# A causal attention and two feed-forward layers on one core: a reordered opening with its softmax sums on TensorE

## The chip, the cores and the metric

The program runs on one NeuronCore of a Trainium2 chip. The metric is the device time of one execution in microseconds (us). The engines are named as in the profile: PE is TensorE (matmuls; PEld its weight loads), DVE is VectorE, ACT is ScalarE, POOL is GpSimd, SP is SyncE, which issues the DMAs.

## What is computed

Two sequences (B = 2) of 576 tokens with 8 heads of 64 columns go through attention with a memory, then through two feed-forward layers. Cut to what matters here:

```python
scores = where(causal, -1e9, q @ k.T / 8)
a = exp(scores - scores.max(-1))
local = (a / (a.sum(-1) + 1e-9)) @ v
phi = lambda x: where(x > 0, x, exp(x) - 1) + 1
mem_out = (phi(q) @ M_prev) / (phi(q) @ z_prev + 1e-6)
g = 1 / (1 + exp(-beta))
x = g * mem_out + (1 - g) * local
x = relu(x @ w_in)**2 @ w_out
out = sum over e of p[:, e] * (relu(x @ w1[e]) @ w2[e])
```

## The kernel before

The 1152 tokens lie in nine tiles of 128. They go through the attention in three chunks: chunk 0 holds the first 128 tokens of both sequences (tiles 7 and 8), chunk 1 four tiles, chunk 2 three. The work is staged. The **opening** (function `opening`, called once) computes the attention of chunk 0 whole. Then the first feed-forward layer of chunk 0 (`ffn1(0, ...)`) runs on TensorE with the attention of chunk 1 mixed in between its products (`rest`), then that layer for chunk 1 with the attention of chunk 2, then for chunk 2, and last the four experts.

In the opening and in the stage behind it every engine takes its instructions in the order in which the code issues them. In the opening that order is one string of step names, which `opening` walks through: `c` is a step of the weight conversion, `s0`/`s1` steps of the scores of heads 0 to 3 and 4 to 7, `p0`/`p1` of the feature map phi, `g` of the gates, `m` the products with the memory, `t` the transposition of a block of Exps with its copy out of PSUM, `v` the product with the values, `n`, `k`, `q`, `x`, `o` the normalisation, weighing, addition and transposition into the layer's input, `S` the first scores of chunk 1, `w` the first step of the layer. A block (unit) is one sequence and four heads, 128 queries by 128 keys per head, so there are four blocks.

A head's scores come from PSUM with the mask added and the row maximum taken by VectorE (`top`, L189); ScalarE then takes the Exp of 128 columns at a time (L324) and writes the row sum beside it with `accum_out`, which is an instruction of its own in the trace (ACTIVATION_READ_ACCUMULATOR). VectorE copies three of the four transposed blocks out of PSUM (L339), ScalarE the fourth (L341). phi is one Exp on ScalarE and two operations on VectorE (L181, L183, L184). The weights are the reciprocal of the sums times one minus the gate (L424 to L426), for all heads at once; the weighing (L432) and the addition of the memory's part (L433) go by sequence.

The opening shares ScalarE, VectorE and SyncE with the weight conversion (`convert`): the first layer's weights arrive as 64-bit words, 512 KB per block (`fetch`, L722), ScalarE makes two halves of the number (L734, L737), VectorE joins them (L740, L745), and the result `bits` goes both to TensorE and to a buffer in DRAM (L748). SyncE takes its issues in order, so the load of a later block stands behind the write of an earlier one:

```python
def fetch(i):
    words[i] = wp.tile([P, DM, 2], I32, tag=f"w{i % 2}", name="w64")
    nc.sync.dma_start(out=words[i]..., in_=w1[f, half]...)
...
    nc.sync.dma_start(out=w1s[f, half], in_=bits.bitcast(F32))
```

The first product of the layer (L101, `hpa<-y,bits`) needs both sequences' outputs of the opening (`y`, copied by L438) and the first converted block.

Of the kernel before, what the change touches and what calls it, by code (L numbers as in the profile page):

```python
# [10 lines left out]
F32 = mybir.dt.float32  # L11
# [5 lines left out]
AF = mybir.ActivationFunctionType  # L17
# [4 lines left out]
P = 128  # L22
B, H, S, D = 2, 8, 576, 64
# [14 lines left out]
CHUNKS = [(7, 9), (0, 4), (4, 7)]  # L38
# [14 lines left out]
def attention_then_experts(ctx, tc, qa, ka, va, qc, kc, vc, mz, beta, w1, probs, w2, out):  # L53
# [11 lines left out]
    nc = tc.nc  # L65
# [104 lines left out]
    def gates():  # L170
# [59 lines left out]
    def opening(c0, c1, first_layer):  # L230

        sc = [c0.scores(p, spot) for p, spot in zip(c0.pairs, (("s", 3), ("pv", 2)))]
        ph, gt, later = c0.phis(0), gates(), c1.scores(c1.pairs[0])
        units = [u for p in c0.pairs for u in p]
        steps = dict(
            g=lambda: next(gt), c=lambda: next(cv), w=lambda: next(first_layer), l=lambda: [c1.load(1, n) for n in range(2)], L=lambda: c1.load(1, 2), S=lambda: next(later, None),
            n=c0.norms, k=c0.recall, q=c0.weights,
        )
        for i in range(2):
            steps[f"s{i}"] = lambda i=i: next(sc[i], None)  # L240
            steps[f"p{i}"] = lambda i=i: next(ph[i])
            steps[f"x{i}"] = lambda i=i: c0.local(i)
            steps[f"o{i}"] = lambda i=i: c0.out(i)
        for i, u in enumerate(units):
            steps[f"t{i}"] = lambda u=u, e=nc.vector if i < 3 else None: c0.turn(u, e)
            steps[f"v{i}"] = lambda u=u: c0.values(u)
        for i in range(3):
            steps[f"m{i}"] = lambda i=i: c0.states(i)


        order = (
            "c l c L s0 p0 p0 g g p1 s1 s0 s0 s0 s1 s1 p1 m0 t0 s1 t2 s0 s1 m1 m2 n t1 v0 v2 k q x0 "
            "t3 c v1 v3 S o0 x1 o1 c S S c w S S S"
        )
        for k in order.split():
            steps[k]()

    def attention_a(c, pool, eng, banks):


        pairs = []
# [22 lines left out]

        def phis(r):
            e = q[r][1] = pool.tile([P, H, P], F32, tag="phia", name="phia", bufs=2)
            return [phi(e[:, hs], e[:, hs], q[r][0][:, hs]) for hs in (slice(0, 4), slice(4, 8))]

        def s_(pair, spot=None):
            scs = {}  # L290
            tag, bufs = spot or ("s", banks[1])
            for u in pair:
                t, kn, h0, nh = u
                b = TILES[t][0][0]
                if h0 + b == 0:
# [48 lines left out]
        def v_(u):  # L344
            t, kn, h0, nh = u
            b = TILES[t][0][0]
            at = at_.pop(u)
# [47 lines left out]
            b = TILES[t][0][0]  # L395
            finish(t, xls[t - b][:, b], banks[0], banks[2])()

        pms, fs = [], [pool.tile([P, B, H], F32, name=f"f{i}", bufs=1) for i in range(2 * (c == 0))]
        third = (slice(0, 3), slice(3, 6), slice(6, 8))

        def states(i):
            ps, tag, bufs = (banks[0], "m", banks[2]) if i < 2 else (ps_h, "h", 1)
            pms.append(ps.tile([P, 3, B, D + 1], F32, tag=tag, name="pm", bufs=bufs))
            for k, h in enumerate(range(third[i].start, third[i].stop)):
                nc.tensor.matmul(pms[i][:, k], lhsT=q[0][1][:, h, :], rhs=mzd[:, h], start=True, stop=True)

        def norms():
            for pm, hs in zip(pms, third):
                n = hs.stop - hs.start
                nc.vector.tensor_scalar_add(fs[1][:, :, hs], pm[:, 0:n, :, D].rearrange("p h b -> p b h"), 1e-6)  # L410
            nc.vector.reciprocal(out=fs[1], in_=fs[1])
            nc.vector.tensor_mul(fs[1], fs[1], gate[:, None, :].to_broadcast([P, B, H]))

        def recall():
            for pm, hs in zip(pms, third):
                n = hs.stop - hs.start
                nc.vector.tensor_mul(
                    q[0][2][:, :, hs, 0:D].rearrange("p b h d -> p h b d"), pm[:, 0:n, :, 0:D],
                    fs[1][:, :, hs].rearrange("p b h -> p h b")[:, :, :, None].to_broadcast([P, n, B, D]),
                )  # L420

        def weights():
            for b in range(B):
                nc.vector.tensor_scalar_add(fs[0][:, b], st[CHUNKS[0][0] + b][2], 1e-9)  # L424
            nc.vector.reciprocal(out=fs[0], in_=fs[0])
            nc.vector.tensor_mul(fs[0], fs[0], gate1[:, None, :].to_broadcast([P, B, H]))  # L426

        def local(b):
            xl = xls[b] = pool.tile([P, H, D], F32, tag="xl0", name="xl0", bufs=2)
            for i in range(2):  # L430
                hs = slice(4 * i, 4 * i + 4)
                nc.vector.tensor_mul(xl[:, hs], pvs[CHUNKS[0][0], i][:, b], fs[0][:, b, hs, None].to_broadcast([P, 4, D]))  # L432
            nc.vector.tensor_add(xl, xl, q[0][2][:, b, :, 0:D])  # L433
# [809 lines left out]
```

## Time and profile before

| | |
|---|---|
| time, median of 3 runs | 689.8 us (689.16 to 690.34) |
| the profiled execution's own time | 696.75 us |
| its span | 694.6 us |
| busy share of the span | PE 96%, PEld 70%, DVE 74%, ACT 64%, POOL 20% |
| first product of the layer (end of the opening) | 21.72 us |

The span runs from the first to the last instruction of one profiled execution. A timeline row gives the start, the duration, the engine, the line of the program, the operation and what it writes and reads; in brackets stands how long the engine stood idle before it, and what ended that. TensorE's records are passes: an fp32 matmul shows as two, a transposition as one.

### The profile page before, as it was taken

The page shows a single profiled execution, that of the slowest core. Times are in us where ns is not written, and L with a number is a line of the kernel's source. Part 1 is how long each engine was busy: PE and PEld are TensorE (multiplying, and loading weights), DVE is VectorE, ACT ScalarE, POOL GpSimd, SP SyncE. Part 2 cuts the span into 40 slices and gives each one's busy share as a digit, 9 for nine tenths or more (in the row PEclk, how much of TensorE's full clock was granted, in tenths as well). Part 3 has the DMA queues.
Part 4 walks back from the last instruction along what each step waited for, and adds up shares of the span by engine and source line. Part 5 has one row for each costly group of instructions (what it writes and reads, how often), then busy time and mean ns, then how long its engine had stood idle before and what let it go on. Part 6 is the DMA issues. An engine that isn't in the chain of part 4 may idle for free. (4 is left out here: it accounts for less than half of the span.)

```text
span 694.6 us, 12446 instructions
## 1 busy us (share of the span) xinstructions
PE 669.6 (96%) x4604; PEld 483.6 (70%) x4604; DVE 513.4 (74%) x1011; ACT 442.6 (64%) x830; POOL 141.6 (20%) x197
## 2 busy tenths in 40 slices
PE   7799999899999999999999999999999999999997
PEld 4588878677877879999766666656655555555553
DVE  7879787599996586779689679787765856665743
ACT  5689976798686448966888677545534435353430
POOL 1010010000000022004335443433332242423200
PEclk9999999999999999999999999999999999999999
DMA  8798875679955636965122332333341323000002
GB/s 292 259 345 299 283 264 171 210 210 254 259 130 129 120 86 215 328 213 156 62 91 92 122 122 69 127 110 122 107 136 62 103 81 96 25 1 1 1 1 76
DMA packets 65565, 101.24 MB, mean 146 GB/s; under 512 B 32673, under 2 KB 34977, under 8 KB 65505
## 3 DMA queue, kind: packets, MB, share of 16 engines
q1 hardware_dynamic: 65216, 100.32, 47.2%
q8 instruction: 36, 0.59, 0.3%
q14 instruction: 25, 0.20, 0.1%
q10 hardware_dynamic: 288, 0.14, 0.1%
HBM read 82.87 MB, written 10.75 MB: 135 GB/s over the span
## 5 line engine op out<-in xcount | busy, mean ns | idle before, releaser
L1115 PE MATMUL o<-w,g 128*128 128x512 f16 x864 | 216.9, 379 | 0.0
L1017 PE MATMUL pe<-xs,wu 128*128 128x256 f16 (+1 forms) x1344 | 196.2, 286 | 3.1 <-DVE u L1039 2.3
L1017 PEld LDWEIGHTS <-wu 128*128 128x128 f16 x1344 | 130.8, 98 | 72.1 <-issue 6.2
L1115 PEld LDWEIGHTS <-g 128*128 128x128 f16 x864 | 84.5, 98 | 67.7 <-issue 0.2
L1033 ACT ACTIVATE g<-h 128x512 f16<-128x512 f32 (+1 forms) x64 | 43.4, 678 | 106.8 <-DVE h L1039 100.6
L804 PE MATMUL y<-g,w 128*128 128x512 f32 (+1 forms) x384 | 88.9, 369 | 0.7 <-DVE w L84 0.7
L983 POOL TENSOR_TENSOR ws<-raw 128x256 f32<-128x256 f32 x32 | 24.6, 769 | 259.1 <-DVE wu L980 132.9
L804 PEld LDWEIGHTS y<-g,w 128*128 128x128 f32 x384 | 68.2, 188 | 8.0 <-DVE w L84 1.0
L1034 DVE SCALAR_TENSOR_TENSOR g<-h,g 128x512 f16<-128x512 f32 (+1 forms) x64 | 51.6, 806 | 23.3 <-ACT g L1033 23.0
L1039 DVE SCALAR_TENSOR_TENSOR u<-pe,p 128x256 f32<-128x256 f32 (+1 forms) x64 | 28.8, 451 | 37.4 <-PE pe L1017 35.9
L106 PE MATMUL hpb<-x,w 128*128 128x512 f32 x192 | 53.0, 411 | 1.2 <-DVE r L788 1.2
L84 DVE TENSOR_TENSOR w<-wraw,w 128x512 fp32r<-128x512 f32 x64 | 45.3, 715 | 10.5 <-ACT w L83 10.4
L1039 DVE SCALAR_TENSOR_TENSOR h<-pe,u 128x256 f32<-128x256 f32 (+1 forms) x64 | 29.0, 453 | 29.9 <-PE pe L1017 29.6
L83 ACT ACTIVATE w<-wraw 128x512 fp32r<-128x512 f32 x64 | 39.6, 625 | 17.7 <-PE y L804 10.5
L980 DVE SCALAR_TENSOR_TENSOR wu<-ws,wpow,wu 128x512 f16<-128x512 f32 x64 | 45.6, 750 | 1.9 <-ACT wu L991 1.9
L189 DVE CUSTOM_DVE_ANT_0 a<-sc,mask 128x384 f32<-128x384 f32 (+4 forms) x80 | 36.5, 479 | 14.1 <-PE sc L589 9.9
L925 DVE SCALAR_TENSOR_TENSOR w<-raw,wpow,w 128x1024 f16<-128x1024 f32 x32 | 41.4, 1294 | 1.8 <-ACT w L924 1.3
L106 PEld LDWEIGHTS hpb<-x,w 128*128 128x128 f32 x192 | 35.5, 193 | 9.8 <-DVE r L788 2.4
L991 ACT ACTIVATE wu<-ws,wpow 128x1024 f16<-128x1024 f32 x32 | 36.4, 1137 | 6.4 <-POOL ws L988 6.4
L985 ACT ACTIVATE wu<-raw,wpow 128x768 f16<-128x768 f32 x32 | 29.8, 932 | 13.4 <-PE pe L1017 11.5
L980 DVE SCALAR_TENSOR_TENSOR wu<-raw,wpow,wu 128x768 f16<-128x768 f32 x32 | 33.2, 1039 | 6.1 <-ACT wu L985 5.7
L924 ACT ACTIVATE w<-raw,wpow 128x1024 f16<-128x1024 f32 x32 | 36.3, 1134 | 0.0
(172 smaller groups left out, 1101.9 us busy)
## 6 DMA issues: line engine op xcount, KB each, us to landing
raw<-in_w SPq DMA_DIRECT2D x64, 512.0 KB, 3.7
w<-in_w SPq DMA_DIRECT2D x32, 512.0 KB, 5.4
wraw<-w1s SPq DMA_DIRECT2D x64, 256.0 KB, 3.2
w1s<-bits SPq DMA_DIRECT2D x32, 256.0 KB, 3.7
kraw<-in_kc SPq DMA_DIRECT2D x8, 576.0 KB, 4.8
vraw<-in_vc SPq DMA_DIRECT2D x8, 320.0 KB, 3.7
qraw<-in_qc SPq DMA_DIRECT2D x4, 512.0 KB, 4.6
out<-acc SPq DMA_DIRECT2D x7, 256.0 KB, 2.0
```

The costliest lines, as they stand in the source:

```text
L83: nc.scalar.activation(out=w[:, 0], in_=raw, func=AF.Copy)
L84: eng.tensor_sub(w[:, 1], raw, w[:, 0].bitcast(F32))
L106: nc.tensor.matmul(acc, lhsT=w[:, a, kk * P:(kk + 1) * P], rhs=xs_r[c][:, b, kk, :], start=(i == 0), stop=(i == 3 * NK - 1),)
L189: nc.vector.tensor_tensor_reduce(out=dst, in0=sc, in1=msk, op0=ALU.add, op1=ALU.max, scale=1.0, scalar=-3.0e38, accum_out=m)
L804: nc.tensor.matmul(yacc[d], lhsT=w[:, a, d * P:(d + 1) * P], rhs=g[:, b], start=(first and i == 0), stop=(last and i == 2),)
L925: nc.vector.scalar_tensor_tensor(out=w1, in0=x, scalar=s, in1=w0, op0=ALU.mult, op1=ALU.subtract)
L980: nc.vector.scalar_tensor_tensor(out=w[:, 1, ks], in0=x, scalar=s1, in1=w[:, 0, ks], op0=ALU.mult, op1=ALU.subtract)
L1017: nc.tensor.matmul(acc, lhsT=w[:, wa, k, kk * P:kk * P + P], rhs=x[:, xb, kk], start=(m == 0 and not onto), stop=(m == 5), skip_group_chec ...
L1033: nc.scalar.activation(out=g[:, 0], in_=hm, func=AF.Relu)
L1034: nc.vector.scalar_tensor_tensor(out=g[:, 1], in0=hm, scalar=0.0, in1=g[:, 0], op0=ALU.max, op1=ALU.subtract)
L1039: nc.vector.scalar_tensor_tensor(out=out, in0=acc, scalar=HID, in1=x, op0=ALU.mult, op1=ALU.add)
L1115: nc.tensor.matmul(outs[t], lhsT=gs[i, m][:, gb, r:r + P], rhs=wds[i, m][:, wa], start=(p == 0 and m == 0 and wa == gb), stop=(p == 3 and ...
```

## The change

Six things change, all in the opening.

1. **Sums.** The Exps of chunk 0 no longer write their row sums. The sums come from TensorE: for each head the transposed block of Exps is loaded as weights and multiplied with one column of ones (`sums`, steps `z0` and `z1`), 8 products per step. The 16 result columns lie at the end of the PSUM bank of the first memory product.
2. **phi.** `phi_first` computes phi(q) of chunk 0 as exp(-relu(-q)) + relu(q): three activations on ScalarE and one addition, which goes to GpSimd for both halves.
3. **Copies.** All four transposed blocks are copied out by ScalarE.
4. **Weights per half.** The weights and the weighing go by four heads and both sequences (`weights(i)`, `local(i)`), so the first half can be weighed before the second is summed.
5. **Additions.** The memory's part is added by sequence in a step of its own (`join`): sequence 0 on VectorE, sequence 1 on GpSimd.
6. **Order.** The string of steps is new: the gates stand first, both phi steps ahead of the Exps, and one more conversion ahead of the layer's input.

```diff
+    def phi_first(out, r, q, eng):
+        nc.scalar.activation(out=out, in_=q, func=AF.Relu, scale=-1.0)
+        nc.scalar.activation(out=out, in_=out, func=AF.Exp, scale=-1.0)
+        nc.scalar.activation(out=r, in_=q, func=AF.Relu)
+        yield
+        eng.tensor_add(out, out, r)
+        yield
...
-            steps[f"t{i}"] = lambda u=u, e=nc.vector if i < 3 else None: c0.turn(u, e)
+            steps[f"t{i}"] = lambda u=u: c0.turn(u)
...
-            "c l c L s0 p0 p0 g g p1 s1 s0 s0 s0 s1 s1 p1 m0 t0 s1 t2 s0 s1 m1 m2 n t1 v0 v2 k q x0 "
-            "t3 c v1 v3 S o0 x1 o1 c S S c w S S S"
+            "g g c s0 l c L p0 p1 p0 s1 s0 s0 s0 s1 s0 s1 m0 t0 p1 s1 m1 m2 n t1 s1 "
+            "v0 t2 v1 z0 q0 k x0 t3 c v2 v3 z1 q1 x1 y1 S y0 S c w o0 o1 S S c S S"
...
+                return [phi_first(e[:, hs], p[:, hs], q[r][0][:, hs], eng) for hs, eng in zip(halves, (nc.gpsimd, nc.gpsimd))]
...
-                        accum_out=sm[:, h0 + i:h0 + i + 1],
+                        accum_out=sm[:, h0 + i:h0 + i + 1] if c else None,
...
+        def sums(i):
+            for u in pairs[i]:
+                at, b = at_.pop(u), TILES[u[0]][0][0]
+                for h in range(4):
+                    nc.tensor.matmul(
+                        sms[CHUNKS[0][0]][:, b, 4 * i + h:4 * i + h + 1], lhsT=at[:, h * P:h * P + P], rhs=ones[:, 0:1],
+                        start=True, stop=True,
+                    )
...
+        def weights(i):
+            hs = slice(4 * i, 4 * i + 4)
+            cf = cfs[i] = pool.tile([P, B, 4], F32, tag="cg", name="cg", bufs=2)
+            nc.vector.tensor_scalar_add(cf, sms[CHUNKS[0][0]][:, :, hs], 1e-9)
+            nc.vector.reciprocal(out=cf, in_=cf)
+            nc.vector.tensor_mul(cf, cf, gate1[:, None, hs].to_broadcast([P, B, 4]))
+
+        def local(i):
...
+            nc.vector.tensor_mul(
+                xls[0][:, :, 4 * i:4 * i + 4], pvs[CHUNKS[0][0], i], cfs[i][:, :, :, None].to_broadcast([P, B, 4, D])
+            )
+
+        def join(b):
+            (nc.gpsimd if b else nc.vector).tensor_add(xls[0][:, b], xls[0][:, b], q[0][2][:, b, :, 0:D])
```

How the instructions stand is shown at three places. `x8` behind a row means eight such instructions in a row; what an instruction waits for stands in brackets.

TensorE, before, from the third block's transposition on (`atp` is a transposed block of Exps, `pv` the product with the values):

```order
L336 MATMUL atp<-ident,a 128x128 [waits Activation_49] x4
L356 MATMUL pv<-va_0_162,at 64x64 [waits DMAHW7_49,DVE_49]
L356 MATMUL pv<-va_0_162,at 64x64 x7
L356 MATMUL pv<-va_0_162,at 64x64 [waits DVE_49]
L356 MATMUL pv<-va_0_162,at 64x64 x7
L336 MATMUL atp<-ident,a 128x128 [waits PE_49,Activation_49]
L336 MATMUL atp<-ident,a 128x128 [waits Activation_49] x3
L356 MATMUL pv<-va_0_164,at 64x64 [waits DMAHW0_49,DVE_49]
L356 MATMUL pv<-va_0_164,at 64x64 x7
L356 MATMUL pv<-va_0_164,at 64x64 [waits DVE_49,Activation_49]
L356 MATMUL pv<-va_0_164,at 64x64 x7
```

TensorE now, from the third block's transposition on:

```order
L352 MATMUL atp<-ident,a 128x128 [waits Activation_49] x4
L372 MATMUL pv<-va_0_163,at 64x64 [waits DMAHW0_49,Activation_49]
L372 MATMUL pv<-va_0_163,at 64x64 x7
L430 MATMUL pm<-ones,at 128x1 [waits DVE_49]
L430 MATMUL pm<-ones,at 128x1 x7
L352 MATMUL atp<-ident,a 128x128 [waits PE_49,Activation_49]
L352 MATMUL atp<-ident,a 128x128 [waits Activation_49] x3
L372 MATMUL pv<-va_0_161,at 64x64 [waits Activation_49]
L372 MATMUL pv<-va_0_161,at 64x64 x7
L372 MATMUL pv<-va_0_163,at 64x64 [waits Activation_49]
L372 MATMUL pv<-va_0_163,at 64x64 x7
L430 MATMUL pm<-ones,at 128x1 [waits DVE_49]
```

The one-column products (L430, writing into the bank `pm`) stand between the first half's values and the fourth block's transposition, and again behind the last values; each step of the values now waits for a copy by ScalarE.

VectorE, before, from the first weighing to the first conversion (`xl` is a sequence's output, `f` the weights, `bits` a converted block):

```order
L432 TENSOR_TENSOR xl_321<-pv,f_149 128x256 [waits DVE_49,PE_49]
L432 TENSOR_TENSOR xl_321<-pv,f_149 128x256 [waits PE_49]
L433 TENSOR_TENSOR xl_321<-xl_321,xm 128x512 [waits DVE_49]
L432 TENSOR_TENSOR xl_377<-pv,f_149 128x256 [waits PE_49] x2
L433 TENSOR_TENSOR xl_377<-xl_377,xm 128x512 [waits DVE_49]
L740 SCALAR_TENSOR_TENSOR bits<-mag,bits 128x512 [waits Activation_49]
L745 SCALAR_TENSOR_TENSOR bits<-w_167,bits 128x512 [waits DMAHW1_49,DVE_49]
L189 ISA a,mx<-sc,mask 128x256 [waits PE_49]
```

VectorE now, from the second half's weights on:

```order
L453 TENSOR_SCALAR cg<-pm 128x8 [waits PE_49]
L454 RECIPROCAL cg<-cg 128x8 [waits DVE_49]
L455 TENSOR_TENSOR cg<-cg,gate_91 128x8 [waits DVE_49]
L460 TENSOR_TENSOR xl<-pv,cg 128x2x256 [waits DVE_49]
L465 TENSOR_TENSOR xl<-xl,xm 128x512 [waits DVE_49]
L198 ISA a,mx<-sc,mask 128x256 [waits PE_49]
L198 ISA mx 128x1
L198 ISA a,mx<-sc,mask 128x256
L198 ISA mx 128x1
L334 TENSOR_SCALAR nb<-mx 128x2 [waits DVE_49]
L772 SCALAR_TENSOR_TENSOR bits<-mag,bits 128x512 [waits Activation_49]
L777 SCALAR_TENSOR_TENSOR bits<-w_171,bits 128x512 [waits DMAHW1_49,DVE_49]
```

One addition has gone to GpSimd, the second half's weights wait for TensorE's sums, and the first row maxima of chunk 1 have moved ahead of the first conversion.

ScalarE, before, from phi's first half on:

```order
L181 ACTIVATE phia<-qa 128x512 [waits DMAHW2_49]
L172 ACTIVATE bt<-bt 128x8 [waits DMAHW0_49]
L181 ACTIVATE phia<-qa 128x512 [waits DMAHW4_49]
L324 ACTIVATE a,sm<-a,nb 128x128 [waits DVE_49]
L324 ACTIVATE a,sm<-a,nb 128x128 x3
L324 ACTIVATE a,sm<-a,nb 128x128 [waits DVE_49]
L324 ACTIVATE a,sm<-a,nb 128x128 x7
L324 ACTIVATE a,sm<-a,nb 128x128 [waits DVE_49]
L324 ACTIVATE a,sm<-a,nb 128x128 x3
L341 ACTIVATE at<-atp 128x512 [waits DVE_49,PE_49]
```

ScalarE now, from the same place:

```order
L181 ACTIVATE phia<-qa 128x512 [waits DMAHW2_49]
L182 ACTIVATE phia<-phia 128x512 [waits Activation_49]
L183 ACTIVATE phip<-qa 128x512
L181 ACTIVATE phia<-qa 128x512 [waits DMAHW4_49]
L182 ACTIVATE phia<-phia 128x512 [waits Activation_49]
L183 ACTIVATE phip<-qa 128x512
L340 ACTIVATE a<-a,nb 128x128 [waits DVE_49]
L340 ACTIVATE a<-a,nb 128x128 x3
L340 ACTIVATE a<-a,nb 128x128 [waits DVE_49]
L340 ACTIVATE a<-a,nb 128x128 x3
L357 ACTIVATE at<-atp 128x512 [waits PE_49]
```

Both halves of phi, three activations each, now stand ahead of all Exps, and the copies of the transposed blocks (L357) stand between the Exps.

On SyncE one issue has moved: the first reload of a converted block for the layer of chunk 1 (L765, `wraw<-w1s`) was the third issue behind the opening and now stands 26 issues later.

## Rows read from the trace of the kernel before

**Rows 1.** Windows: busy us (count) of PE, PEld, DVE, ACT, POOL; granted clock; DMA; GB/s.

```profile
15.00:22.00 7.00, 4.58 (x77) 3.85 (x74) 6.72 (x19) 3.50 (x9) 0.00 (x0) 1.00 0.69 238
...
38.00:40.00 2.00, 2.00 (x26) 1.88 (x24) 0.70 (x2) 2.00 (x7) 0.00 (x0) 0.50 1.03 405
...
126.00:128.00 2.00, 2.00 (x6) 1.51 (x6) 0.00 (x0) 1.60 (x7) 0.47 (x8) 0.50 0.28 58
```

**Rows 2.** Timeline of ScalarE (start us, us, what), opening.

```profile
8.21 0.63 ACT L181 ACTIVATE phia<-qa 128x512 f32<-128x512 f32 x1 [2.65 <-DMA qa<-in_qa]
8.74 0.38 ACT L324 ACTIVATE a<-a,nb 128x128 f32<-128x128 f32 x1
9.04 0.18 ACT L324 ACTIVATION_READ_ACCUMULATOR a<-a,nb 128x1 f32 x1
...
16.07 0.60 ACT L341 ACTIVATE at<-atp 128x512 f32<-128x512 f32 x1 [0.68 <-PE atp L336]
16.57 0.65 ACT L734 ACTIVATE mag<-w 128x512 f32<-128x512 f32 x1
```

**Rows 3.** Timeline of TensorE, opening; a record is one matmul pass.

```profile
12.53 1.40 PE L405 MATMUL pm<-mzd,phia 128*128 128x130 f32 x10
13.77 0.60 PE L336 MATMUL atp<-ident,a 128*128 128x128 f32 x4
14.30 1.15 PE L356 MATMUL pv<-va,at 128*64 128x64 f32 x32
...
21.72 0.48 PE L101 MATMUL hpa<-y,bits 128*128 128x256 f32 x1 [0.74 <-ACT y L438]
```

**Rows 4.** Timeline of VectorE, from the opening's last addition.

```profile
19.42 0.69 DVE L433 TENSOR_TENSOR xl<-xl,xm 128x512 f32<-128x512 f32 x1
20.03 0.68 DVE L740 SCALAR_TENSOR_TENSOR bits<-mag,bits 128x512 int32<-128x512 int32 x1
...
21.35 0.42 DVE L189 CUSTOM_DVE_ANT_0 a<-sc,mask 128x256 f32<-128x256 f32 x1
...
22.24 0.42 DVE L189 CUSTOM_DVE_ANT_0 a<-sc,mask 128x256 f32<-128x256 f32 x1
...
34.59 0.69 DVE L184 SCALAR_TENSOR_TENSOR phia<-qa,phia 128x512 f32<-128x512 f32 x1
```

**Rows 5.** Groups of instructions by line, VectorE, 20 to 36 us; idle time last.

```profile
L740 DVE SCALAR_TENSOR_TENSOR bits<-mag,bits 128x512 int32<-128x512 int32 x7 | 4.8, 686 | 1.9 <-ACT bits L737 1.9
```

**Rows 6.** Timeline of VectorE, 46 to 53 us: softmax weights and weighing of a later half.

```profile
46.24 0.17 DVE L382 TENSOR_SCALAR cg<-sm 128x8 f32<-128x8 f32 x1
...
46.67 0.17 DVE L384 TENSOR_TENSOR cg<-cg,gate 128x8 f32<-128x8 f32 x1
...
52.66 0.68 DVE L391 TENSOR_TENSOR xl<-pv,cg 128x512 f32<-128x512 f32 x1
```

**Rows 7.** Timelines of ScalarE and TensorE, around the halt after 32 us.

```profile
31.56 0.66 ACT L734 ACTIVATE mag<-w 128x512 f32<-128x512 f32 x1 [2.93 <-DMA w<-in_w]
...
35.33 0.94 PE L365 MATMUL pm<-mzd,phia 128*128 128x130 f32 x6 [3.07 <-DVE phia L184]
...
36.63 1.98 PE L356 MATMUL pv<-va,at 128*64 128x64 f32 x32
38.54 1.85 PE L307 MATMUL sc<-ka,qa 64*128 64x128 f32 x16
```

**Rows 8.** DMA issues of SyncE at 24.97 us, the last column us to landing.

```profile
w<-in_w SPq DMA_DIRECT2D x1, 512.0 KB, 6.5
```

**Rows 9.** Timeline of TensorE, two other halts.

```profile
8.32 1.16 PE L307 MATMUL sc<-ka,qa 64*128 64x128 f32 x16 [1.79 <-DMA qa<-in_qa]
...
123.97 0.66 PE L197 MATMUL tp<-ident,xl 128*128 128x128 f32 x4 [1.98 <-DVE x L206]
```

**Rows 10.** Timelines of GpSimd and VectorE, the same microseconds.

```profile
48.21 2.49 POOL L377 TENSOR_TENSOR xm<-xm,cf 128x512 f32<-128x512 f32 x2 [43.99 <-DVE cf L375]
...
48.49 1.30 DVE L740 SCALAR_TENSOR_TENSOR bits<-mag,bits 128x512 int32<-128x512 int32 x1 [0.47 <-ACT bits L737]
```

More of the change, by code (lines that the diff above doesn't have):

```diff
@@ L236, in opening @@
             g=lambda: next(gt), c=lambda: next(cv), w=lambda: next(first_layer), l=lambda: [c1.load(1, n) for n in range(2)], L=lambda: c1.load(1, 2), S=lambda: next(later, None),
-            n=c0.norms, k=c0.recall, q=c0.weights,
+            n=c0.norms, k=c0.recall,
         )
@@ L241, in opening @@
             steps[f"p{i}"] = lambda i=i: next(ph[i])
+            steps[f"q{i}"] = lambda i=i: c0.weights(i)
+            steps[f"z{i}"] = lambda i=i: c0.sums(i)
             steps[f"x{i}"] = lambda i=i: c0.local(i)
+            steps[f"y{i}"] = lambda i=i: c0.join(i)
             steps[f"o{i}"] = lambda i=i: c0.out(i)
         for i, u in enumerate(units):
-            steps[f"t{i}"] = lambda u=u, e=nc.vector if i < 3 else None: c0.turn(u, e)
+            steps[f"t{i}"] = lambda u=u: c0.turn(u)
             steps[f"v{i}"] = lambda u=u: c0.values(u)
@@ L286, in phis @@
             e = q[r][1] = pool.tile([P, H, P], F32, tag="phia", name="phia", bufs=2)
-            return [phi(e[:, hs], e[:, hs], q[r][0][:, hs]) for hs in (slice(0, 4), slice(4, 8))]
+            halves = slice(0, 4), slice(4, 8)
+            if r == 0:
+                p = pool.tile([P, H, P], F32, name="phip", bufs=1)
+                return [phi_first(e[:, hs], p[:, hs], q[r][0][:, hs], eng) for hs, eng in zip(halves, (nc.gpsimd, nc.gpsimd))]
+            return [phi(e[:, hs], e[:, hs], q[r][0][:, hs]) for hs in halves]
         def s_(pair, spot=None):
@@ L294, in s_ @@
                 b = TILES[t][0][0]
-                if h0 + b == 0:
+                if h0 + b == 0 and c:
                     sms[t] = pool.tile([P, B, H], F32, tag="sm", name="sm", bufs=2)
                 if h0 == 0:
-                    st[t] = [pool.tile([P, H], F32, tag=x, name=x, bufs=4) for x in ("mx", "nb")] + [sms[t - b][:, b]]
+                    st[t] = [pool.tile([P, H], F32, tag=x, name=x, bufs=4) for x in ("mx", "nb")] + [sms[t - b][:, b] if c else None]
                 scs[u] = banks[0].tile([P, 512], F32, tag=tag, name="sc", bufs=bufs)
@@ L346, in v_ @@
             b = TILES[t][0][0]
-            at = at_.pop(u)
+            at = at_.pop(u) if c else at_[u]
             half = t - b, h0 // 4
@@ L396, in stand @@
             finish(t, xls[t - b][:, b], banks[0], banks[2])()
-        pms, fs = [], [pool.tile([P, B, H], F32, name=f"f{i}", bufs=1) for i in range(2 * (c == 0))]
+        pms, fn = [], pool.tile([P, B, H], F32, name="fn", bufs=1) if c == 0 else None
         third = (slice(0, 3), slice(3, 6), slice(6, 8))
@@ L402, in states @@
             ps, tag, bufs = (banks[0], "m", banks[2]) if i < 2 else (ps_h, "h", 1)
-            pms.append(ps.tile([P, 3, B, D + 1], F32, tag=tag, name="pm", bufs=bufs))
+            room = ps.tile([P, 512], F32, tag=tag, name="pm", bufs=bufs)
+            pms.append(room[:, 0:3 * B * (D + 1)].rearrange("p (h b d) -> p h b d", h=3, b=B))
+            if i == 0:
+                sms[CHUNKS[0][0]] = room[:, 512 - B * H:].rearrange("p (b h) -> p b h", b=B)
             for k, h in enumerate(range(third[i].start, third[i].stop)):
                 nc.tensor.matmul(pms[i][:, k], lhsT=q[0][1][:, h, :], rhs=mzd[:, h], start=True, stop=True)
+        def sums(i):
[6 more added lines that the diff above has]
+                    )
         def norms():
@@ L409, in norms @@
                 n = hs.stop - hs.start
-                nc.vector.tensor_scalar_add(fs[1][:, :, hs], pm[:, 0:n, :, D].rearrange("p h b -> p b h"), 1e-6)
-            nc.vector.reciprocal(out=fs[1], in_=fs[1])
-            nc.vector.tensor_mul(fs[1], fs[1], gate[:, None, :].to_broadcast([P, B, H]))
+                nc.vector.tensor_scalar_add(fn[:, :, hs], pm[:, 0:n, :, D].rearrange("p h b -> p b h"), 1e-6)
+            nc.vector.reciprocal(out=fn, in_=fn)
+            nc.vector.tensor_mul(fn, fn, gate[:, None, :].to_broadcast([P, B, H]))
         def recall():
@@ L418, in recall @@
                     q[0][2][:, :, hs, 0:D].rearrange("p b h d -> p h b d"), pm[:, 0:n, :, 0:D],
-                    fs[1][:, :, hs].rearrange("p b h -> p h b")[:, :, :, None].to_broadcast([P, n, B, D]),
+                    fn[:, :, hs].rearrange("p b h -> p h b")[:, :, :, None].to_broadcast([P, n, B, D]),
                 )
[L422 to L433, printed above, removed]
+        def weights(i):
[5 more added lines that the diff above has]
+        def local(i):
+            if i == 0:
+                xls[0] = pool.tile([P, B, H, D], F32, tag="xl", name="xl", bufs=2)
+            nc.vector.tensor_mul(
[3 more added lines that the diff above has]
+            (nc.gpsimd if b else nc.vector).tensor_add(xls[0][:, b], xls[0][:, b], q[0][2][:, b, :, 0:D])
         def out_(b):
             tp = banks[0].tile([P, NK, P], F32, tag="m", name="tp", bufs=banks[2])
-            upright(tp, xls[b])
+            upright(tp, xls[0][:, b])
             nc.scalar.activation(out=first_x[:, :, b * P:b * P + P], in_=tp, func=AF.Copy)
@@ L441, in attention_a @@
             pairs=pairs, load=load, load_v=load_v, phis=phis, scores=s_, turn=t_, values=v_, mem=mem, recalled=recalled, weigh=weigh, blend=blend, stand=stand,
-            states=states, norms=norms, recall=recall, weights=weights, local=local, out=out_,
+            states=states, sums=sums, norms=norms, recall=recall, weights=weights, local=local, join=join, out=out_,
         )
```

## The prediction

> **What bounds the kernel now.** I read the windows first, then the timelines of ScalarE, TensorE and VectorE through the opening, then the halts of TensorE behind it. In the opening the window from 15 to 22 us shows VectorE busy for 6.72 of 7 us and TensorE for 4.58 [rows 1]: VectorE carries the end. Its last addition starts at 19.42 and hands over at 20.03 [rows 4]; the first product of the layer starts at 21.72 [rows 3].
>
> Yet that start is not what the rest of the time hangs on. TensorE stands still once more: 3.07 us before 35.33, for VectorE's phi of chunk 1, and that in turn waited for ScalarE, which stood 2.93 us for a block of weights until 31.56 [rows 7]. Behind this halt the granted clock is 0.50 from 38 to 40 us, which is 1.2 of 2.4 GHz [rows 1]. From 40 us on TensorE works through its order with hardly a gap, so I take a shift of its restart at 35.33, and of the work just behind it, as a shift of the end. The question is therefore when VectorE and the weights let TensorE restart, and whether the clock falls.
>
> **The change, part by part: the opening.** *phi.* ScalarE begins its second half at 8.21, when q lands, and goes on 0.53 later, at 8.74 [rows 2]. Now the first Relu must end (0.63) before its Exp, and the Exp and the second Relu each let the next start after 0.53: the first softmax Exp moves from 8.74 to 9.90. GpSimd's two additions cost about 1.25 each (2.49 for two of that size [rows 10]); they lie under ScalarE's Exps and cost nothing, since TensorE's second memory products start at 12.53 today [rows 3] and the sum is there by 11.3. If that cover went, those products would be late by as much. The first half lies under the wait for q, and the gates, now first, lie there too.
>
> *Exps and copies.* An Exp occupies 0.30 before its sum's read begins at 9.04 [rows 2], and nothing else is left of it, so four take 1.20. A copy takes 0.60 and lets the next start after 0.50 [rows 2]. Hence: first block to 11.10, second to 12.30, copy to 12.80, third to 14.00, the second copy ready at 14.60, fourth block to 15.70, third copy ready at 16.30. The 16 reads saved are worth about what the added copies and activations cost.
>
> *The one-column products.* No row shows one. Each step has 8 fp32 products, two passes each, so 16 passes that load 128 columns of weights. Upper bound: the memory products, 10 passes in 1.40, 0.125 apart after the first, 2.0 per step. Lower bound: the value products, 64 columns wide, 32 passes in 1.15, 0.03 apart, 0.5 per step. Nearest are the transpositions, which load the same 128 by 128 of fp32: four in 0.60, 0.11 apart [rows 3]. I take 0.11, 1.76 per step. The Trainium skill, TensorE: Matmul & The Clock Gate, section Back-to-back issue gap, gives a floor of about 25 ns from one product to the next however few its columns; by it a step would cost 0.4 us, an estimate. No row here has so narrow a product.
>
> *The chain to the last addition.* Second block's values on TensorE from 14.65, 0.55 (half of 1.15 [rows 3]), to 15.20; first sums to 16.95; only then the fourth block's transposition, 0.60, to 17.55; its copy, 0.60, to 18.15; its values to 18.70; second sums to 20.45. Then VectorE: weights 0.60 (46.24 to the end of 46.67's), weighing 0.68 [rows 6], to 21.75; the addition hands over 0.61 later (19.42 to 20.03 [rows 4]), at **22.35 instead of 20.03: 2.3 us late**. What VectorE lost (two halves of phi, three copies, one addition) no longer lies on the path: TensorE's sums took its place. With 0.03 a pass the fourth block's Exps bind instead, and the same chain ends at 20.0; with 0.125 at 22.85. The recall and the first weighing fit while VectorE waits for the second sums.
>
> The first product then waits for the first conversion too, which the new order puts behind a set of row maxima: 0.89 (21.35 to 22.24), then 1.32 (20.03 to 21.35 [rows 4]), at 24.6 against 21.72. Both conversions of that stretch are only swapped with the maxima; nothing of it is added.
>
> **The change, part by part: the restart.** From the hand-over at 20.03 to the end of phi at 35.28 (34.59 and 0.69 [rows 4]) VectorE has the same instructions in both kernels, in another order. Of these 15.25 us it waited 1.9 for ScalarE [rows 5], so 13.35 is work. From 22.35 this gives 35.70: a restart 0.4 late at least. The weights can make it later. SyncE issues the load that ended at 31.56 once two blocks are converted: 0.89, two times 1.32 and 0.4 after the hand-over, 26.3 (24.97 before). With the 6.5 that it took [rows 8] it lands at 32.8, and with the 3.77 from there to the restart (31.56 to 35.33 [rows 7]) TensorE starts at 36.6, 1.25 late. I take the middle, **0.8 late**, because a reload for the second layer that stood among these issues comes much later now.
>
> **The clock.** TensorE's work ahead of the halt comes about 2.0 later (that stretch hangs on VectorE too), so the halt is some 1.85 instead of 3.07. A halt of 1.79 before 8.32 left the clock at 1.00 afterwards; 1.98 before 123.97 was followed by 0.50 [rows 9, 1]. It stands between them, but the 5 us ahead of it are denser than before, so I say it holds, 6 in 10. Then the value products take 1.15 instead of 1.98 and the scores 1.16 instead of 1.85 [rows 3, 7, 9]: **1.5 gained**.
>
> **Sum.** 0.8 late and 1.5 back is 0.7 less: 696.05 for the profiled execution of 696.75, whose span is 694.6. The runs' median of 689.8 lies 6.95 under it; I carry the difference over: **689.1 us**, no change that can be told (0.2%, 1.4 us, is about what a measurement of this kernel tells from none).
>
> **Rivals.**
> - *Cheap sums.* If a pass costs 0.03, the hand-over stays at 20.0, the load is issued at 23.95 and TensorE restarts at 34.2, 1.1 early. If the clock holds as well, 2.6 in all: 687.2. Against the clock: the halt would be 2.2. Without it 688.7.
> - *The clock falls all the same.* The main chain, with nothing back: 0.8 late, 690.6.
> - *The two additions collide (slower).* Sequence 0's addition on VectorE and sequence 1's on GpSimd are released by the same weighing, and each reads two operands from SBUF. Beside a GpSimd operation a VectorE one of 0.69 took 1.30 [rows 10]. If GpSimd starts first and VectorE waits for all of it, 1.25 more stand before the hand-over and the restart is 2.05 late. The halt stays near 1.85, since the work ahead of it is late as well; if the clock falls as before, 691.8. It decides once the restart is later than the 1.5 that the clock can give back, or once the clock gives nothing back. The Trainium skill, SBUF — State Buffer, section Who interferes with whom, says that of two such instructions the second waits until the first is over; the row agrees only in that it was slowed. If VectorE starts first, GpSimd's addition ends near 23.65, and the layer's input still arrives with the conversion.
> - *It does not end what bounds.* If the restart hangs on the weights alone, the opening's length matters only through their issue; the cases above contain that.
>
> **How the numbers follow.** Main case 0.40; cheap sums 0.25, about half of it with the clock held; clock falls, 0.20; collision 0.15. Faster by over 1.4 takes the half of the second case, and a part of the first (a restart not late at all with the clock held is 1.5 less) and of a mixture in which the passes cost some 0.07: 0.30. Slower by over 1.4 takes the collision and the upper end of the third (1.25 late): 0.22. The rest, 0.48, is within. The range goes from the cheap sums to the collision, 687.2 to 691.8.
>
> **What would show it.** Right: one-column passes about 0.11 apart; VectorE waiting for each of the two sums; the last addition handing over near 22.35 and the first product near 24.6; TensorE's restart near 36, with a halt under 2 us; clock 1.00 from 36 to 41. Wrong: passes 0.03 to 0.06 apart; an addition of sequence 0 of over 1 us; a halt of 3 us again; or a shift that is seen at 41 us and gone by 120, which would mean that the stage behind the opening is not bound by TensorE.

## The result and the profile after

The changed kernel takes **694.53 us** (median of 4 runs, 693.65 to 694.79); the kernel before, beside it, 689.48 (4 runs, 688.93 to 690.34). The ratio is 1.0063, with a 95% interval of 1.0049 to 1.0078: **5.05 us slower**, above the range forecast (687.2 to 691.8), where 0.7 us less had been forecast. The profiled execution took 694.29 us, its span is 692.2.

The windows of the changed kernel, columns as in [rows 1]:

```profile
14.00:16.00 2.00, 2.00 (x23) 1.94 (x18) 0.00 (x0) 1.04 (x3) 0.00 (x0) 1.00 1.02 394
16.00:18.00 2.00, 2.00 (x27) 1.67 (x27) 1.88 (x7) 1.11 (x3) 0.00 (x0) 0.50 1.05 401
20.00:22.00 2.00, 2.00 (x11) 2.00 (x11) 0.00 (x0) 0.00 (x0) 0.00 (x0) 0.50 0.04 15
24.00:26.00 2.00, 1.85 (x11) 1.26 (x8) 1.97 (x7) 0.43 (x1) 1.40 (x1) 0.50 0.00 0
26.00:28.00 2.00, 1.31 (x7) 0.93 (x6) 1.93 (x5) 1.66 (x7) 0.00 (x0) 0.94 0.20 72
38.00:41.00 3.00, 2.95 (x50) 2.55 (x52) 2.93 (x6) 3.00 (x11) 0.00 (x0) 1.00 0.94 313
```

TensorE counts as busy all the time from 14 to 24 us, and yet the granted clock is 0.50, 1.2 of 2.4 GHz, from 16 us on; it is back only at 26. Before, TensorE was busy for 4.58 of 7 us from 15 to 22 and the clock stood at 1.00 [rows 1]. VectorE, which carried the end there, now does nothing from 20 to 22.

Its timeline of TensorE, opening and restart:

```profile
14.06 1.95 PE L430 MATMUL pm<-ones,at 128*128 128x1 f32 x16
15.87 0.98 PE L352 MATMUL atp<-ident,a 128*128 128x128 f32 x4
16.79 1.98 PE L372 MATMUL pv<-va,at 128*64 128x64 f32 x32
18.69 3.58 PE L430 MATMUL pm<-ones,at 128*128 128x1 f32 x16
22.20 2.08 PE L323 MATMUL sc<-ka,qa 64*128 64x128 f32 x16
...
38.05 0.94 PE L381 MATMUL pm<-mzd,phia 128*128 128x130 f32 x6 [1.36 <-DVE phia L193]
...
39.35 1.15 PE L372 MATMUL pv<-va,at 128*64 128x64 f32 x32
```

The first step of sums ran at 1.00: 16 passes from 14.06 to 15.87, 0.113 apart. The second took 3.58, 0.22 a pass, and the values and scores around it take 1.98 and 2.08, where 1.15 and 1.16 are their time at full clock [rows 3], [rows 9]. The restart, 35.33 in [rows 7], is at 38.05; its halt is 1.36 instead of 3.07, and behind it the clock holds (value products 1.15, not 1.98).

Its timeline of ScalarE, where the second half of q lands:

```profile
7.12 0.63 ACT L181 ACTIVATE phia<-qa 128x512 f32<-128x512 f32 x1 [0.54 <-DMA qa<-in_qa]
```

Before, that stood at 8.21 [rows 2]. In the profiled executions of kernels with this order of the first steps it lies between 6.8 and 8.2 us, so the head start of 1.1 us here is not a sure one.

Its timelines of VectorE and of GpSimd:

```profile
16.05 0.17 DVE L453 TENSOR_SCALAR cg<-pm 128x8 f32<-128x8 f32 x1 [3.75 <-PE pm L430]
...
22.30 0.17 DVE L453 TENSOR_SCALAR cg<-pm 128x8 f32<-128x8 f32 x1 [3.79 <-PE pm L430]
...
22.94 0.69 DVE L460 TENSOR_TENSOR xl<-pv,cg 128x512 f32<-128x512 f32 x1
23.67 0.69 DVE L465 TENSOR_TENSOR xl<-xl,xm 128x512 f32<-128x512 f32 x1
24.30 0.42 DVE L198 CUSTOM_DVE_ANT_0 a<-sc,mask 128x256 f32<-128x256 f32 x1
...
23.71 1.69 POOL L465 TENSOR_TENSOR xl<-xl,xm 128x512 f32<-128x512 f32 x1 [13.44 <-DVE xl L460]
```

VectorE waits for both steps of sums, 7.5 us in all, and hands over at 24.30 instead of 20.03 [rows 4]. The two additions don't collide on VectorE: sequence 0's takes its 0.69 beside GpSimd's of 1.69 (longer than the 1.25 of [rows 10]). The layer's first product starts at 27.16 instead of 21.72 [rows 3].

### The profile page after: what moved, and what is told of

Same layout as the page of the kernel before. It is cut to its first block, busy times and chain, and to the rows that moved or that the text cites. A ratio compares the mean times of both kernels' runs of the same rounds, so it can differ in the third digit from the quotient of the medians.

```text
span 692.2 us, 12493 instructions
## 1 busy us (share of the span) xinstructions
PE 674.4 (97%) x4636; PEld 488.7 (71%) x4636; DVE 509.9 (74%) x1003; ACT 445.6 (64%) x821; POOL 145.3 (21%) x200
## 5 line engine op out<-in xcount | busy, mean ns | idle before, releaser
L1015 POOL TENSOR_TENSOR ws<-raw 128x256 f32<-128x256 f32 x32 | 24.6, 768 | 259.8 <-DVE wu L1012 132.9
L1066 DVE SCALAR_TENSOR_TENSOR g<-h,g 128x512 f16<-128x512 f32 (+1 forms) x64 | 51.7, 808 | 23.1 <-ACT g L1065 22.9
L106 PEld LDWEIGHTS hpb<-x,w 128*128 128x128 f32 x192 | 34.4, 188 | 9.6 <-DVE r L820 2.4
L1012 DVE SCALAR_TENSOR_TENSOR wu<-raw,wpow,wu 128x768 f16<-128x768 f32 x32 | 33.3, 1041 | 6.0 <-ACT wu L1017 5.7
```

The source lines that it names most:

```text
L106: nc.tensor.matmul(acc, lhsT=w[:, a, kk * P:(kk + 1) * P], rhs=xs_r[c][:, b, kk, :], start=(i == 0), stop=(i == 3 * NK - 1),)
L1012: nc.vector.scalar_tensor_tensor(out=w[:, 1, ks], in0=x, scalar=s1, in1=w[:, 0, ks], op0=ALU.mult, op1=ALU.subtract)
L1066: nc.vector.scalar_tensor_tensor(out=g[:, 1], in0=hm, scalar=0.0, in1=g[:, 0], op0=ALU.max, op1=ALU.subtract)
```

## The experiments

Each was compared with runs of the kernel before on the same chip. Theory A, from the profile: the opening is late because TensorE's clock falls around the one-column products. Rivals: their weight loads cost as much at any width (B); GpSimd's addition, phi on ScalarE or the later issue of the layer's weights do it (C). A kernel's time comes from several executions, its profile from one of them.

**1. The kernel before, again.** No edit.

> The kernel before, profiled once more, since its first profiled execution stood 7 us above its median. If that execution was untypical through its 1.98 us halt at 122 to 124 and the two stretches at half clock (36.6 to 40.2 and 125.7 to 129 us), the new profile has a time within 1 us of 689.5, and one or both of the stretches are gone. If they are there again, the 7 us lie elsewhere. In the opening both theories expect the old picture: granted clock 1.00 from 15 to 22 us, last addition handing over near 20.0, first layer product near 21.7.

Measured: 690.89 us, 1.0003 of before (0.9979 to 1.0026); the profiled execution 691.79. A row of its timeline of TensorE and two windows:

```profile
8.28 1.89 PE L307 MATMUL sc<-ka,qa 64*128 64x128 f32 x16 [2.01 <-DMA qa<-in_qa]
...
36.00:38.00 2.00, 2.00 (x13) 1.35 (x12) 1.93 (x5) 2.00 (x8) 0.00 (x0) 0.50 1.05 414
...
120.00:124.00 4.00, 4.00 (x22) 3.31 (x21) 1.86 (x3) 2.08 (x6) 0.17 (x5) 1.00 0.26 68
```

The halt of 1.98 before 123.97 [rows 9] and the half clock behind it are gone, and with them 3.7 us (VectorE's same instructions stand 0.1 apart in the two executions at 115 us, 3.8 at 131); that was one execution's. The half clock from 36 us is there again, behind a halt of 2.58 at 35.52. In the opening it is new: 0.50 from 8.5 to 11.9 us, behind the halt of 2.01 before 8.28, without any narrow product. From 15 to 22 us the clock is 1.00, and the first product starts at 22.39, 0.7 after the 21.72 of the first profile.

**2. The sums read on ScalarE again**, all else changed:

```diff
-                        accum_out=sm[:, h0 + i:h0 + i + 1] if c else None,
+                        accum_out=sm[:, h0 + i:h0 + i + 1],
...
-                at, b = at_.pop(u), TILES[u[0]][0][0]
-                for h in range(4):
-                    nc.tensor.matmul(
...
+                at_.pop(u)
```

> The changed kernel with the Exps' sums read on ScalarE again and no one-column products; all other parts of the change stay. Theory A (the one-column products, and the granted clock that falls to 0.50 with them, make the opening late): granted clock 1.00 from 16 to 26 us, last addition handing over at 19 to 21 instead of 24.30, first layer product at 20.5 to 23 instead of 27.16, time 4 to 6 us under the changed kernel, 688.5 to 690.5. Theory C (GpSimd's addition, phi on ScalarE or the weights issued late make it): the opening stays at least 3 us late, time at or over 692.5.

Measured: 690.09 us, 0.9992 (0.9971 to 1.0013). The 5 us are the one-column products and what they bring; the rest of the change costs nothing (C falls). The handing over is at 20.16. The clock, though, did not hold all through: it was 0.50 from 22.9 to 26.3 us. Timeline of TensorE:

```profile
21.34 0.66 PE L206 MATMUL tp<-ident,xl 128*128 128x128 f32 x4 [0.38 <-POOL xl L458]
22.77 3.63 PE L101 MATMUL hpa<-y,bits 128*128 128x256 f32 x8 [0.78 <-DVE bits L770]
...
35.03 0.94 PE L381 MATMUL pm<-mzd,phia 128*128 128x130 f32 x6 [1.37 <-DVE phia L193]
```

Eight products at half clock, 3.63 instead of 1.99 before, behind halts of 0.43, 0.38 and 0.78 and without any narrow product near. So the products aren't the only way to lose the clock.

**3. The sums 64 columns wide**, in a PSUM tile of their own; column 0 is read:

```diff
...
-                        sms[CHUNKS[0][0]][:, b, 4 * i + h:4 * i + h + 1], lhsT=at[:, h * P:h * P + P], rhs=ones[:, 0:1],
-                        start=True, stop=True,
+                        sms[i][:, b, h], lhsT=at[:, h * P:h * P + P], rhs=ones[:, 0:D], start=True, stop=True,
...
```

> The changed kernel with each sum taken by a product of 64 equal columns instead of one, so that the weight loads stay and the columns grow. Theory A (what costs is mostly the clock, which falls while TensorE works on products one column wide): granted clock 1.00 or near it from 16 to 26 us, each of the two steps of 16 passes about 2.0 us, handing over near 22.3, time 691 to 692.5. Theory B (the 16 weight loads of a step cost the same at any width, and the clock falls just as well): steps of about 2.0 and 3.6 us again, handing over at 24.3 or later, time 694 to 695.

Measured: 692.06 us, 1.0016 (0.9996 to 1.0035). Timeline of TensorE:

```profile
14.31 2.00 PE L429 MATMUL sums<-ones,at 128*128 128x64 f32 x16
16.14 0.61 PE L352 MATMUL atp<-ident,a 128*128 128x128 f32 x4
16.68 1.45 PE L372 MATMUL pv<-va,at 128*64 128x64 f32 x32
18.05 2.00 PE L429 MATMUL sums<-ones,at 128*128 128x64 f32 x16
...
24.69 1.96 PE L101 MATMUL hpa<-y,bits 128*128 128x256 f32 x8 [0.79 <-DVE bits L775]
...
35.51 0.94 PE L381 MATMUL pm<-mzd,phia 128*128 128x130 f32 x6 [1.37 <-DVE phia L193]
```

and a window:

```profile
18.00:20.00 2.00, 2.00 (x24) 1.88 (x18) 0.81 (x2) 1.63 (x3) 0.00 (x0) 1.00 0.48 104
```

The weight loads of the first step, in the changed kernel and here:

```profile
14.06 1.86 PEld L430 LDWEIGHTS pm<-ones,at 128*128 128x128 f32 x16
...
14.31 1.86 PEld L429 LDWEIGHTS sums<-ones,at 128*128 128x128 f32 x16
```

With 64 times the columns the passes stand 0.114 apart (14.31 to 16.14), as at one column, so the columns don't set the pace. The loads of 128 by 128 weights run without a break for 1.86 us at either width, and I take the pace to be theirs; no run changes the loads alone. But the clock is 1.00 throughout. VectorE hands over at 22.07. From the first sum to the first product it is 10.38 us, against 13.10 (14.06 to 27.16) in the changed kernel; to the restart 21.20 against 23.99. The mean granted clock, listed for every execution that was timed, says the same beyond the profiled ones: 0.986 to 0.995 in all 37 with one-column sums (the changed kernel and the runs 4, 5, 7, 8 and 9), 0.993 to 1.000 with a median of 0.999 in the ten of this run, 0.991 to 1.000 with a median of 0.996 in the 70 of the kernel before.

**4. The old phi for chunk 0** in the changed kernel:

```diff
-            if r == 0:
-                p = pool.tile([P, H, P], F32, name="phip", bufs=1)
...
             return [phi(e[:, hs], e[:, hs], q[r][0][:, hs]) for hs in halves]
```

> The changed kernel with the old phi for chunk 0: one Exp on ScalarE and two operations on VectorE for each half. Theory C (the two further activations of each half hold ScalarE's softmax Exps up and so the whole chain): Exps start 0.8 to 1.2 us earlier, time 1 us or more under the changed kernel, 693.5 or less. Theory A: the chain hangs on TensorE's sums, time within 0.7 us of 694.5, clock still 0.50 from 16 to 26 us.

Measured: 695.84 us, 1.0062 (1.0043 to 1.0082): no gain, and 0.6 us more than theory A allowed. The Exps do start earlier, 1.14 after q lands instead of 1.71, but VectorE, busy with the row maxima, then makes the second half of phi late: TensorE stood 2.30 for it before 12.43. Behind that halt the clock was at 0.50 from 13.9 to 17.3, before any sum; it came back during the first step of sums and was at 0.50 again from 20.7 to 34.4.

**5. The changed kernel, again.** No edit.

> The changed kernel once more, to have its time beside the other experiments and to see whether the half clock is there in another execution. Theory A: granted clock 0.50 again for 8 us or more between 14 and 28 us, second step of sums over 3 us, first layer product at 26 to 28 us, time 3 to 6 us over the kernel before. If the half clock were a matter of one execution, the profile would show 1.00 from 16 to 22 us, sums of 2.0 us each and the first product near 24.7.

Measured: 695.46 us, 1.0060 (1.0043 to 1.0077). Timeline of TensorE:

```profile
14.27 1.95 PE L430 MATMUL pm<-ones,at 128*128 128x1 f32 x16
...
18.24 3.57 PE L430 MATMUL pm<-ones,at 128*128 128x1 f32 x16
...
39.58 0.94 PE L381 MATMUL pm<-mzd,phia 128*128 128x130 f32 x6 [1.36 <-DVE phia L193]
```

Half clock from 17.7 to 31.3; steps of 1.95 and 3.57, first product at 26.80, restart at 39.58, 25.31 from the first sum at 14.27. How long the half clock lasts differs between the two executions; it came in both.

**6. The mix:** reads as in 2 (that edit isn't shown again), both additions on VectorE, and the first conversion ahead of the row maxima:

```diff
-            "v0 t2 v1 z0 q0 k x0 t3 c v2 v3 z1 q1 x1 y1 S y0 S c w o0 o1 S S c S S"
+            "v0 t2 v1 z0 q0 k x0 t3 c v2 v3 z1 q1 x1 S y0 o0 y1 o1 c S w S S c S S"
...
-            (nc.gpsimd if b else nc.vector).tensor_add(xls[0][:, b], xls[0][:, b], q[0][2][:, b, :, 0:D])
+            nc.vector.tensor_add(xls[0][:, b], xls[0][:, b], q[0][2][:, b, :, 0:D])
```

> The changed kernel with the Exps' sums read on ScalarE again, both additions on VectorE, and the first layer's conversions ahead of the row maxima. In the run that only took the one-column products out, TensorE stood 0.43, 0.38 and 0.78 us ahead of 22.77, and the first eight products of the layer then took 3.63 us at clock 0.50 instead of 1.99. Theory: with these halts shorter the clock stays 1.00, the first product starts at 22.2 to 22.5 and the restart at 35.03 is 1 to 2 us earlier: 1 to 2.5 us under that run's 690.1, and 2 us or more under the kernel before. Rival: the weights (SyncE's loads) set the restart whatever the first products do, and it stays within 0.5 us of that run.

Measured: 689.21 us, 0.9979 (0.9964 to 0.9994), faster than before. The first eight products take 1.96 at clock 1.00, the restart comes at 34.54, 0.5 earlier than in the run of 2: less than expected, and within the 0.5 of the rival, though not for its reason: VectorE's phi releases it, and of VectorE's time from 22 to 34 us only 0.28 is waiting. (In this execution the clock was at 0.50 earlier, from 7.3 to 14.1 us, again without a narrow product.)

**7. Both additions on VectorE**, nothing else (the last edit of 6).

> The changed kernel with both additions on VectorE. Theory A: the second addition ends at about 24.9 instead of 25.4, the layer starts 0.3 to 0.6 earlier, time within 0.8 us of the changed kernel, clock 0.50 from 16 us as before. Theory C (GpSimd's 1.69 us addition is a large part of the 5 us): time 1.5 us or more under the changed kernel.

Measured: 695.16 us, 1.0058 (1.0040 to 1.0077): GpSimd's addition is no part of the 5 us. Its profiled execution began the sums late, at 15.11, and had the half clock from 17.3 to 34.4 us; the first product is at 28.45.

**8. The one-column sums alone**, put into the kernel before:

```diff
-            "c l c L s0 p0 p0 g g p1 s1 s0 s0 s0 s1 s1 p1 m0 t0 s1 t2 s0 s1 m1 m2 n t1 v0 v2 k q x0 "
-            "t3 c v1 v3 S o0 x1 o1 c S S c w S S S"
+            "c l c L s0 p0 p0 g g p1 s1 s0 s0 s0 s1 s1 p1 m0 t0 s1 t2 s0 s1 m1 m2 n t1 v0 v1 z0 k "
+            "t3 c v2 v3 z1 q x0 S o0 x1 o1 c S S c w S S S"
...
-                nc.vector.tensor_scalar_add(fs[0][:, b], st[CHUNKS[0][0] + b][2], 1e-9)
+                nc.vector.tensor_scalar_add(fs[0][:, b], sms[CHUNKS[0][0]][:, b], 1e-9)
...
```

> The kernel before with one part of the change alone: sums by one-column products instead of ScalarE's reads, with the weights behind the second step of sums; phi, copies, gates and additions as before. Theory A (the narrow products make the clock fall whatever stands around them): granted clock 0.50 for 5 us or more between 15 and 28 us, second step of sums over 3 us, first layer product at 25 to 28, time 3 us or more over the kernel before. Theory B (it takes the rest of the new order too, which packs TensorE's work closer): clock 1.00, steps of 2.0 us, first product near 24, 1 to 2.5 us over.

Measured: 697.89 us, 1.0093 (1.0071 to 1.0115). Timeline of TensorE:

```profile
19.51 1.95 PE L415 MATMUL pm<-ones,at 128*128 128x1 f32 x16
21.39 1.16 PE L308 MATMUL sc<-ka,qa 64*128 64x128 f32 x16
23.81 1.12 PE L197 MATMUL tp<-ident,xl 128*128 128x128 f32 x4 [1.25 <-DVE xl L446]
...
27.06 3.78 PE L101 MATMUL hpa<-y,bits 128*128 128x256 f32 x8 [0.69 <-ACT y L451]
```

and two windows:

```profile
20.00:22.00 2.00, 2.00 (x24) 1.99 (x25) 0.47 (x3) 0.00 (x0) 0.00 (x0) 1.00 0.04 12
22.00:24.00 2.00, 0.75 (x11) 0.56 (x10) 1.90 (x6) 0.00 (x0) 0.00 (x0) 0.76 0.00 0
```

Neither forecast of this run is whole. Both steps took 1.95 at clock 1.00, against A; it fell only at 23.0, after the second step and in the halt that VectorE's weights and weighing now make behind it. From there to 33.3 it is 0.50, the first product is at 27.06, and the time 2.4 us over the whole change's beside it (695.46 in the run of 5). So narrow products needn't be slow themselves: the half clock can come just behind them. In the run of 3 a halt of 1.06 stood at the same place, behind 64-column sums, and the clock held; whether the 1.25 here would have cost it without narrow products, no run shows.

**9. One column, in the tile of 3:** only the width differs from that run. Shown against that run's line:

```diff
...
-                        sms[i][:, b, h], lhsT=at[:, h * P:h * P + P], rhs=ones[:, 0:D], start=True, stop=True,
+                        sms[i][:, b, h, 0:1], lhsT=at[:, h * P:h * P + P], rhs=ones[:, 0:1], start=True, stop=True,
...
```

> The changed kernel with its one-column products written to the tile of PSUM that the 64-column products used, so that only the width differs from that run. Theory A (the width): granted clock 0.50 for 8 us or more between 15 and 30 us, second step of sums over 3 us, time 694 to 696 as the changed kernel. Rival (the sums' place in the bank of the memory products made the difference, not the width): clock 1.00 from 16 to 22 us, steps of 2.0 us, first product near 24.7, time near 692.

Measured: 694.57 us, 1.0054 (1.0034 to 1.0074). A window of it, and the second step of sums in its timeline of TensorE:

```profile
20.00:22.00 2.00, 2.00 (x12) 1.99 (x13) 0.38 (x3) 0.00 (x0) 0.00 (x0) 0.50 0.04 12
```

```profile
17.94 3.57 PE L429 MATMUL sums<-ones,at 128*128 128x1 f32 x16
```

The width decides, not the place in PSUM. B falls: the loads are the same at both widths, the clock is not.

**10. The mix, with the second conversion ahead of the row maxima too.** Order, against the changed kernel:

```diff
-            "v0 t2 v1 z0 q0 k x0 t3 c v2 v3 z1 q1 x1 S y0 o0 y1 o1 c S w S S c S S"
+            "v0 t2 v1 z0 q0 k x0 t3 c v2 v3 z1 q1 x1 S y0 y1 c w o0 o1 S S c S S S"
```

> The mix again, with the layer's second conversion ahead of the row maxima too. In the mix TensorE stood 1.31 us ahead of 25.76, since the maxima that free its tile came behind a conversion that itself waited 0.28 us for ScalarE; now the maxima follow the two conversions without that wait. VectorE's work up to phi of chunk 1 binds the restart at 34.54 then: 0.3 us earlier at most, time within 0.8 us of the mix's 689.2.

Measured: **689.0 us, 0.9974 (0.9963 to 0.9985): 1.0 to 2.6 us faster than before**, the best here, and level with the mix. Timeline of TensorE:

```profile
21.45 1.97 PE L101 MATMUL hpa<-y,bits 128*128 128x256 f32 x8 [0.76 <-ACT y L463]
24.34 1.16 PE L323 MATMUL sc<-ka,qa 64*128 64x128 f32 x16 [0.93 <-DVE mx L198]
...
33.13 0.94 PE L381 MATMUL pm<-mzd,phia 128*128 128x130 f32 x6 [1.37 <-DVE phia L193]
```

The clock is 1.00 from 14 to 41 us in this execution. The restart is 1.41 earlier than in the run of 6, where 0.3 at most was expected; 0.9 of that is q, which landed at 7.21 here and at 8.12 there.

**11. Phi of chunk 1 as for chunk 0**, on top of 10 (`if r < 2:` for `if r == 0:`).

> The last one, with phi of chunk 1 as three activations on ScalarE and an addition on GpSimd, as the change makes it for chunk 0. If VectorE's work (two operations of 0.42 and 0.69 us for each half) is what the restart at 34.54 waits for, the 1.36 us halt goes and the products behind it start 0.8 to 1.3 us earlier: 688 to 688.8. If ScalarE's wait for the weights (1.81 us until 33.26) binds instead, phi is late and the time stays at or over 689.2.

Measured: 690.87 us, 1.0001 (0.9991 to 1.0011): the gain is gone. Timelines of VectorE, GpSimd and TensorE:

```profile
32.22 1.65 DVE L770 SCALAR_TENSOR_TENSOR bits<-w,bits 128x512 int32<-128x512 int32 x1
...
31.67 1.64 POOL L185 TENSOR_TENSOR phia<-phia,phip 128x512 f32<-128x512 f32 x1 [20.39 <-ACT phip L183]
...
33.36 0.94 PE L381 MATMUL pm<-mzd,phia 128*128 128x130 f32 x6 [0.70 <-POOL phia L185]
...
39.92 0.94 PE L381 MATMUL pm<-mzd,phia 128*128 128x130 f32 x6 [1.52 <-ACT xm L384]
```

The halt at the restart did shrink, from 1.37 to 0.70. But VectorE's conversion that met GpSimd's addition took 1.65 instead of 0.69, and a new halt of 1.52, for ScalarE (which has the additional activations), stands before 39.92. Here the collision that the forecast feared is seen, at another place than feared.

## Why the prediction was wrong

**The price of the sums: right.** 1.76 us for a step of 16 passes, from 0.11 a pass; measured 1.81 at full clock, at one column as at 64. The rival of cheap sums is gone with it. The estimate of 0.4 us, from the floor in the Trainium skill's TensorE: Matmul & The Clock Gate, section Back-to-back issue gap, does not fit these products: the section gives that floor for a product by itself, and here each brings its own 128 by 128 fp32 weights.

**The chain and the restart: near as long as the clock holds, in part by luck.** In the run with 64 columns VectorE hands over at 22.07 and the first product starts at 24.69; forecast were 22.35 and 24.6. But q had landed by 7.01 there, 1.2 before the 8.21 of the forecast, and the first sums began at 14.31 instead of 15.20. From there to the hand-over the chain took 7.76, forecast were 7.15: two errors cancel. Forecast from the hand-over to the restart were 13.8 us (22.35 to 36.15), the middle between VectorE's work (13.35) and the weights; it took 13.44 there, without a wait of VectorE, and 13.75 in the changed kernel, with one of 0.27 for ScalarE. So the work binds, and the weights add nothing. The halt came out under 2 us, and the clock held behind it, as forecast: the 1.5 us that this gives back are in the trace.

**The step that failed** is the clock in the opening. The prediction put the clock into one place only, the halt before the restart; for the chain of the opening it took full-clock prices throughout and gave no reason for that; none of its rows has so narrow a product. The windows show TensorE busy all the time by the profile, and the clock at 0.50 for 10 us. The second step of sums then took 3.58 for 1.81, the hand-over came at 24.30, 1.95 after the forecast, and the first product at 27.16, 2.56 after; as q landed 1.1 earlier than the forecast took it, the chain itself lost more than these two show. No rival contained this; the nearest, "the clock falls all the same", spoke of the restart alone. The experiments on the width price it: changed kernel and one-column run stand at 1.0060 and 1.0054 of before, the 64-column run at 1.0016, some 3 us less; by the timelines the way from the first sum to the restart is 2.8 us longer in the first execution of the changed kernel and 4.1 in the second.

**The rest of the 5 us** is the price of the sums themselves: from reads (0.9992) to 64-column products with the clock held (1.0016) it is 0.24%, about 1.7 us, with intervals that overlap; no trace follows it to the end. The forecast had this as 0.8 late, and against it the 1.5 from the clock. The run with reads restarts at 35.03, the clock holds behind that, and its median is level with before.

**The base** was an untypical execution: 3.7 of the 6.95 us by which it stood over the runs were lost between 119 and 131 us. Carrying the difference over took for granted that the half clock behind the restart, on which the gain rested, is there in the other runs too. It came again in the second profile of before, but 7 of the 70 timed executions of before list a mean clock of 1.000, so it is not there in all.

**The collision** came the harmless way round. VectorE's addition started first (23.67 against 23.71) and kept its 0.69; GpSimd's took 1.69 and ended 1.10 after the hand-over, at 25.40, where the forecast had 1.30 for this case. The run of 7, without it, is no faster.

What stays open: why passes that count as busy don't hold the clock; why the half clock ends at 26 us in one execution of the changed kernel and at 31 in the other; and some 1.5 us that the changed kernel loses behind 140 us against the second profile of before. The run of 10, without narrow products, loses 0.8 of them too, between 300 and 345 us, at a halt of TensorE of 0.7 that the first profile of before also has, so that part is not the change's.

## What to carry to other kernels

A matmul pass that streams one column counts as busy in the profile, yet TensorE's clock can fall to half during it or just behind it, and then the wide work around it takes nearly twice as long (scores 2.08 for 1.16). Before moving small sums to TensorE, price them by the weight load (0.113 us per 128 by 128 fp32 pass here) and look at what the granted clock does there: the same sums at 64 columns cost nothing more per pass, and the clock held in the profiled execution. Where a read beside ScalarE's Exp does the job, leave it.

## What the runs showed of the hardware

- Passes with 128 by 128 fp32 weights stand 0.113 us apart with one column and 0.114 with 64, at full clock; with one column 0.22 at half clock.
- The granted clock was 0.50 while the profile shows TensorE busy 2.00 of 2.00 us, window after window from 16 to 24 us; in all six profiled executions with one-column sums it fell behind the start of the first step, between 16 and 23 us, and was down until 26 to 34. In the seven without them it was 1.00 from 14.1 to 22.8.
- A VectorE operation of 0.69 us took 1.65 beside a GpSimd addition that had begun first (31.67 against 32.22), and 0.69 where it began first itself (23.67 against 23.71); then the GpSimd addition took 1.69 instead of 1.25 [rows 10].
